# A list scheduler that plans VectorE's SBUF operations and GpSimd's operations in turns

## The chip, the cores and the metric

The kernel runs on one core of a Trainium2 chip. The core has a matrix engine (TensorE, PE in the profile), three engines for elementwise work (VectorE or DVE, ScalarE or ACT, GpSimd or POOL), an engine that issues most of the transfers (SyncE or SP), and 16 DMA engines. Each engine takes its own instructions strictly in the order in which the program lists them, and waits where one needs a result that is not there yet. The metric is the device time of one execution in microseconds, as the median of the runs. VectorE, ScalarE and TensorE reach the accumulators (PSUM, eight banks); GpSimd works in this kernel only between tiles of the on-chip memory (SBUF).

## What is computed

The reference is a windowed attention followed by a two-layer feed-forward block:

```python
scores = (1 / sqrt(64)) * q @ k.T            # 4 batches, 8 heads, 768 positions, 64 wide
keep = is_sink | ((rel >= 0) & (rel < 128))  # the first 4 positions, or the last 128
a = softmax(where(keep, scores, -1e9))
x = concat_heads(a @ v)                      # 3072 tokens x 512
h = x @ w_in                                 # 512 x 2048
g = h * sigmoid(1.702 * h)
out = g @ w_out                              # 2048 x 512, float32
```

All inputs are float32. The kernel casts them to float16 on the chip and accumulates in float32.

## The kernel before

The 3072 tokens are worked through in twelve blocks k = 0 to 11 of 256 tokens (three blocks make a batch). For each block and each of four pairs of heads p there is a *front*: q and k are cast to float16 (tiles qk), transposed on TensorE (L446), copied out of PSUM (qkT), multiplied to scores (L513), put through the exponential on ScalarE (L530, tiles at) and multiplied by a 0/1 mask on VectorE (L539, or L543 for the first block of a batch). Then there is a *back*: TensorE multiplies by v (L573), VectorE takes the reciprocal of the sums and scales (L587, L589, tiles xn), and TensorE transposes the result (L596) into xT. For the first block of a batch GpSimd also copies the keys and values of the sink positions (ks, L466, and vs, L422).

The first layer, `mm1`, multiplies xT by w_in in eight groups of eight matmuls per block (L630). Of each group ScalarE takes tanh (L642, tiles th), VectorE builds gT from th and the PSUM bank (L644), and the bank is free again. Three such banks rotate.

The second layer, `mm2`, multiplies gT by w_out. Blocks 0, 1 and 11 do so directly (L780). Blocks 2 to 10 use a scheme that replaces eight products of halves by seven (L705). It needs four tiles wt, which are sums and differences of quarters of w_out (`sums`, L650 to L660): 4 tiles x 4 pieces = 16 operations of 128 x 512 elements. A piece c needs the casts c and 4 + c of w_out, of eight. It also needs four sums of gT per block (sm, L675, on VectorE).

Weights come in as eight loads of 1 MB (w0 to w3 are w_in, w4 to w7 w_out, in the order w4, w6, w5, w7), each into one of four staging places that lie in the tiles gT and sm. Each load is followed by two casts of 128 x 1024 elements; all sixteen are on GpSimd (`CAST_W`). The casts of q, k and v are on GpSimd from k = 2 on; for k = 0 and 1 the planner may choose among engines (`CAST_QK`, `CAST_V`). All casts have one line in the profile, L263.

The order on every engine is found by a planner that runs before the kernel is built (`Plan.run`, L57). Each operation is given one or several engines with two planned times: how long it occupies the engine, and how long until its result is there. The planner keeps the time at which each engine is free, and takes operations one by one: for each engine it finds the earliest start, picks, among operations that could start within 20 ns of it, the one of the lowest priority number, and then takes the engine whose choice comes first. Where an operation may go to several engines, the later end counts against an engine (L120). Priorities are due times: `nominal(k, slot)` is 9000 + 16600 k + 16600 slot / 8 ns. The sums of w_out have the due time of k = 2; the casts of weights come before everything. The planned times in question are:

```python
"POOL": (n / 0.96 + 30, n / 0.96 + 130), "DVE": (n / 1.92 + 40, n / 1.92 + 155),   # casts of n
"ACT": (n / 1.2 + 60, n / 1.2 + 170)
SUM_W = {"POOL": (1000, 1100), "DVE": (340, 430)}                                  # a sum of w_out
```

so a cast of 1024 is planned with 1097 ns on GpSimd and 913 on ScalarE (results after 1197 and 1023), and a cast of 512 with 563 on GpSimd. In the plan every engine works on its own: an operation of VectorE takes the same planned time whether GpSimd is working or not. The planned times set only the order of the instructions; the waits on the chip follow from the data alone.

Of the kernel before, what the change touches and what calls it, by code (L numbers as in the profile page):

```python
# [35 lines left out]
LANES = 8  # L36

COLD = 4700.0
ENGINES = ("PE", "ACT", "DVE", "POOL", "SP")


class Plan:
# [14 lines left out]
    def run(self, warm=None, warm_until=0.0, late_bank=0.0):  # L57
        for o in self.ops:
            o.left = len(o.deps)
            for d in o.deps:  # L60
                d.users.append(o)
        free = {e: 0.0 for e in ENGINES}
        ready = {e: [o for o in self.ops if e in o.engs and not o.left] for e in ENGINES}

        bank_free = {b: 0.0 for b in range(self.n_banks)}
        if late_bank:
            bank_free[self.n_banks - 1] = late_bank

        count = {c: {i: 0.0 for i in range(n)} for c, n in self.limits.items()}
        dma_free = 0.0  # L70
        landed = []
        order = []
        todo = len(self.ops)

        def after(d, e):
            if d.eng != e or isinstance(d.engs[e][1], tuple):
                return d.end + HOP.get((d.eng, e), 50)
            return d.start + d.engs[e][0] + (0 if d.eng == "PE" else 60)

        def could(o, e):  # L80

            if o.behind and o.behind.start is None:
                return None, None
            s = max([free[e]] + [after(d, e) for d in o.deps])
            if isinstance(o.engs[e][1], tuple) and len(landed) >= LANES:
                s = max(s, landed[-LANES])
            if not o.acq:
                return s, s
            cls, n = o.acq
            times = sorted(bank_free.values())  # L90
            places = sorted(count[cls].values())
            if len(times) < n or len(places) < n:
                return s, None
            return s, max(s, times[n - 1], places[n - 1])

        while todo:
            best = None
            for e in ENGINES:
                found = sorted(
                    [(*could(o, e), o) for o in ready[e]], key=lambda x: (x[2].prio, x[2].seq)  # L100
                )
                keep, held_from = [], None
                for s0, s, o in found:
                    if s0 is None:
                        continue
                    if o.acq and o.acq[1] > 2 and (s is None or s > s0):

                        held_from = s0 if held_from is None else min(held_from, s0)
                        if s is not None:
                            keep.append((s, o))  # L110
                        continue
                    if s is None or (o.acq and held_from is not None and s >= held_from):
                        continue
                    keep.append((s, o))
                if not keep:
                    continue
                first = min(s for s, _ in keep)
                s, o = min(((s, o) for s, o in keep if s <= first + 20), key=lambda x: (x[1].prio, x[1].seq))
                lat = o.engs[e][1]
                key = s if len(o.engs) == 1 else s + lat - min(x[1] for x in o.engs.values())  # L120
                if best is None or key < best[0]:
                    best = (key, s, o, e)
            if best is None:
                raise RuntimeError("no operation can be planned")
            _, s, o, e = best
            dur, lat = o.engs[e]
            if e == "PE" and warm and s < warm_until:
                t = max(free["PE"], 300.0)
                while t + 110 < s:
                    order.append((t, -1, warm, e))  # L130
                    t += 107 if t < COLD else 57
            for x in o.engs:
                ready[x].remove(o)
            o.eng, o.start = e, s
            if o.acq:
                cls, n = o.acq
                o.banks, o.places = [], []
                for _ in range(n):
                    b = min((b for b in bank_free if bank_free[b] <= s), key=lambda b: (bank_free[b], b))
                    del bank_free[b]  # L140
                    o.banks.append(b)
                    p = min((p for p in count[cls] if count[cls][p] <= s), key=lambda p: (count[cls][p], p))
                    del count[cls][p]
                    o.places.append(p)
            free[e] = s + dur
            if isinstance(lat, tuple):
                dma_free = max(s + 2000, dma_free) + lat[0]
                o.end = dma_free + (500 if lat[0] < 500 else 1100)
                landed.append(o.end)
            else:  # L150
                o.end = s + lat
            for owner, i in o.rel:
                t = o.end + 80
                bank_free[owner.banks[i]] = t
                count[owner.acq[0]][owner.places[i]] = t
            for u in o.users:
                u.left -= 1
                if not u.left:
                    for x in u.engs:
                        ready[x].append(u)  # L160
            order.append((s, o.seq, o.fn, e))
            todo -= 1
        order.sort(key=lambda x: (x[0], x[1]))
        return [(fn, e) for _, _, fn, e in order]
# [7 lines left out]
def kernel(  # L172
# [38 lines left out]
    mask = pool.tile([P, 4 * P], FP16, name="mask")  # L211
# [7 lines left out]
    wt = {n: pool.tile([P, NH, HM], FP16, name=f"wt{n}") for n in "1234"}  # L219
# [36 lines left out]
    def cast(n, engs):  # L256

        ns = {"POOL": (n / 0.96 + 30, n / 0.96 + 130), "DVE": (n / 1.92 + 40, n / 1.92 + 155),
              "ACT": (n / 1.2 + 60, n / 1.2 + 170)}
        return pick(ns, engs)  # L260

    def copy(e, out, in_):
        {"POOL": nc.gpsimd.tensor_copy, "DVE": nc.vector.tensor_copy, "ACT": nc.scalar.copy}[e](out=out, in_=in_)  # L263
# [3 lines left out]
    def uses(name, slot, o):  # L267
        users.setdefault((name, slot), []).append(o)
# [38 lines left out]
    o_table = op("ACT", 1300, 1400, lambda: nc.scalar.activation(out=dummy, in_=zero[:, 0:8], func=AF.Exp),  # L307
                 [o_zero], prio=NEVER + 8, kind="const")

    CAST_W = ["POOL"] * 8  # L310
    CAST_QK = ["DVE ACT POOL", "DVE POOL"] + ["POOL"] * (NK - 2)
    CAST_V = ["POOL ACT DVE", "POOL ACT"] + ["POOL"] * (NK - 2)
    COPY = ["DVE ACT"] * NK
# [4 lines left out]
    def weights(n_th, j, at):  # L318
# [8 lines left out]
        for n in range(2):  # L327
# [3 lines left out]
            else:  # L331
                to, fr = w_out16[:, 4 * (j - 4) + 2 * n : 4 * (j - 4) + 2 * n + 2], dst[:, 2 * n : 2 * n + 2]
            o = plan.any(cast(1024, CAST_W[j]), lambda e, to=to, fr=fr: copy(e, to, fr), [o_l], prio=at, kind="cw")
            uses(*stage[n_th % RW][:2], o)
# [11 lines left out]
    def nominal(k, slot):  # L346
        return 9000.0 + k * L + slot * L / 8
# [302 lines left out]
    def sums():  # L650

        for n, x, y, alu in (("3", wq["22"], wq["12"], ALU.subtract), ("1", wq["12"], wq["11"], ALU.subtract),
                             ("2", wt["3"], wq["11"], ALU.add), ("4", wq["21"], wt["2"], ALU.subtract)):
            for c in range(4):
# [4 lines left out]
                deps = [o_wout[c], o_wout[NS // 2 + c]] + [o_wt[d, c] for d in {"2": "3", "4": "2"}.get(n, "")]  # L659
                o_wt[n, c] = plan.any(SUM_W, f, deps, prio=nominal(SEVEN_FROM, 0), kind="wt")  # L660

    SUM_W = {"POOL": (1000, 1100), "DVE": (340, 430)}
    o_sm = {}

    def mm2_seven(k):
# [215 lines left out]
```

## Time and profile before

| what | value |
|---|---|
| median of 3 runs | 236.49 us (236.44 to 236.9) |
| the profiled execution | 236.4 us, of it 234.7 us from the first to the last instruction |
| granted TensorE clock, mean | 0.992 |
| TensorE busy | 222.2 us |
| VectorE busy | 190.3 us in 412 instructions |
| ScalarE busy | 140.9 us in 293 instructions |
| GpSimd busy | 98.6 us in 163 instructions |
| the 16 casts of weights, all on GpSimd | 5.2 + 4.5 us (w_in), 4.4 + 4.1 us (w_out) |
| sums of w_out on VectorE, GpSimd | 15 and 1 |

The profile is one execution. Its page gives the busy time of each engine, then the span in 40 equal slices with a digit for the busy tenths of each, the clock that TensorE was granted (9 is full), the chain of work that ended last, and groups of instructions by line. A group shows line, engine, operation, tiles written and read, shape and count, then busy time and mean duration of one, then the idle time of its engine in front of it and what ended that. Matmuls overlap each other, so their durations are longer than their spacing, and a TensorE that is shown as busy is not at its peak.

### The profile page before, as it was taken

What the parts mean: (1) busy time and instruction counts of PE and PEld (TensorE: products, weight loads), DVE (VectorE), ACT (ScalarE), POOL (GpSimd) and SP (SyncE); (2) the same over time, 40 slices, a digit from 0 to 9 for tenths busy, and PEclk for the clock granted to TensorE, in tenths of its full rate; (3) what the DMA queues carried; (4) which work ended last, traced back from release to release, by engine and by line L of the source; (5) the groups of instructions that cost most, each with busy time, mean ns of one, the idle gap of its engine ahead of it and who ended that gap; (6) DMA issues with size and microseconds to landing.
All of it is one profiled execution on the core that took longest, in us unless ns stands there. A gap on an engine that the chain in (4) does not pass through costs nothing.

```text
span 234.7 us, 6390 instructions
## 1 busy us (share of the span) xinstructions
PE 222.2 (95%) x2534; PEld 183.0 (78%) x2534; DVE 190.3 (81%) x412; ACT 140.9 (60%) x293; POOL 98.6 (42%) x163
## 2 busy tenths in 40 slices
PE   8876999959999999999999999999999999999994
PEld 7654886526788888888789889888888888888863
DVE  6788979976899988988979879889969869878520
ACT  3749562536688838838648838838567757635320
POOL 5658889971899960358521441243300000000000
PEclk9999999979999999999999999999999999999999
DMA  6999999999879994644284004004003003003042
GB/s 169 292 357 387 382 383 287 288 302 274 223 191 295 250 232 90 176 100 89 74 197 92 0 3 89 4 1 94 0 13 82 0 14 78 3 17 78 0 92 89
DMA packets 45743, 33.98 MB, mean 145 GB/s; under 512 B 1552, under 2 KB 38672, under 8 KB 45712
## 3 DMA queue, kind: packets, MB, share of 16 engines
q1 hardware_dynamic: 44480, 32.90, 52.0%
q10 hardware_dynamic: 1232, 0.66, 1.0%
q8 instruction: 20, 0.33, 0.6%
q14 instruction: 11, 0.09, 0.1%
HBM read 27.26 MB, written 6.29 MB: 143 GB/s over the span
## 4 chain that ended last, share of the span: by engine, by line
PE 75%; DVE 17%; ACT 3%; DMA 2%; issue 1%; ACTq 0%
PE bank L630 29%; PE bank L705 22%; PE bank L780 6%; PE bank L573 5%; DVE wt L658 5%; PE bank L513 4%; PE bank L446 4%; DVE gT L644 3%; DVE sm L675 2%; PE bank L596 2%; DMA qk<-in_k_dram 2%; DVE at L539 2%; ACT at L530 2%; DVE at L543 1%; PE bank L474 1%
## 5 line engine op out<-in xcount | busy, mean ns | idle before, releaser
L630 PE MATMUL bank<-xT,w_in 128*128 128x256 f16 x768 | 101.7, 273 | 0.0
L642 ACT ACTIVATE th<-bank 128x512 f16<-128x512 f32 x96 | 57.6, 601 | 49.6 <-PE bank L630 46.0
L630 PEld LDWEIGHTS <-w_in 128*128 128x128 f16 x768 | 72.1, 98 | 10.3 <-issue 1.3
L644 DVE SCALAR_TENSOR_TENSOR gT<-th,bank 128x512 f16<-128x512 f16 x96 | 64.9, 679 | 9.0 <-ACT th L642 8.7
L530 ACT ACTIVATE at<-bank 128x512 f16<-128x512 f32 (+1 forms) x96 | 49.1, 569 | 11.8 <-PE bank L513 11.2
L263 POOL CAST qk<-qk 128x512 f16<-128x512 f32 (+1 forms) x42 | 28.9, 722 | 27.9 <-PE bank L446 25.7
L263 POOL CAST v<-v 64x512 f16<-64x512 f32 x43 | 30.3, 705 | 8.8 <-PE bank L573 6.4
L705 PE MATMUL bank<-wt,sm 128*128 128x256 f16 x216 | 30.6, 273 | 0.4 <-DVE sm L675 0.3
L705 PEld LDWEIGHTS <-sm 128*128 128x128 f16 x288 | 26.5, 98 | 4.8 <-DVE sm L675 0.9
L539 DVE TENSOR_TENSOR at<-at,mask 128x1024 f16<-128x1024 f16 x32 | 23.5, 753 | 6.6 <-ACT at L530 6.6
L780 PE MATMUL bank<-w_out,gT 128*128 128x512 f16 (+1 forms) x112 | 24.5, 358 | 0.0
L573 PE MATMUL bank<-v,at 128*128 128x65 f16 x352 | 21.5, 193 | 2.0 <-DVE at L539 1.8
L705 PEld LDWEIGHTS <-gT 128*128 128x128 f16 x216 | 20.1, 98 | 2.3 <-issue 0.3
L573 PEld LDWEIGHTS <-at 128*128 128x128 f16 x352 | 17.3, 97 | 4.0 <-DVE at L539 2.2
L589 DVE TENSOR_TENSOR xn<-bank,rcp 128x256 f16<-128x256 f32 x48 | 19.8, 417 | 0.4
L466 POOL COPY ks<-qkT 64x4 f16<-64x4 f16 x32 | 9.5, 297 | 24.8 <-ACT qkT L263 19.7
L705 PE MATMUL bank<-w_out,gT 128*128 128x256 f16 x144 | 19.7, 273 | 0.0
L446 PE MATMUL bank<-ident,qk 128*128 128x128 f16 x192 | 18.9, 225 | 0.5 <-DVE qk L263 0.4
L730 DVE SCALAR_TENSOR_TENSOR osb<-bank,osb 128x256 f32<-128x256 f32 x45 | 18.4, 409 | 0.6 <-PE bank L705 0.6
L482 ACT ACTIVATE ats<-bank 128x256 f16<-128x256 f32 x32 | 12.4, 388 | 9.2 <-PE bank L474 7.8
L446 PEld LDWEIGHTS <-qk 128*128 128x128 f16 x192 | 14.0, 100 | 3.1 <-DVE qk L263 1.1
L780 PEld LDWEIGHTS <-gT 128*128 128x128 f16 x112 | 10.9, 101 | 6.9 <-issue 1.3
(53 smaller groups left out, 274.4 us busy)
## 6 DMA issues: line engine op xcount, KB each, us to landing
v<-in_v_dram SPq DMA_DIRECT2D x12, 512.0 KB, 7.2
out_dram<-osb SPq DMA_DIRECT2D x45, 128.0 KB, 2.4
qk<-in_q_dram SPq DMA_DIRECT2D x11, 512.0 KB, 5.2
qk<-in_k_dram SPq DMA_DIRECT2D x11, 512.0 KB, 6.7
gT<-in_moe_w_in_dram SPq DMA_DIRECT2D x2, 1024.0 KB, 10.1
sm<-in_moe_w_in_dram SPq DMA_DIRECT2D x2, 1024.0 KB, 13.0
gT<-in_moe_w_out_dram SPq DMA_DIRECT2D x2, 1024.0 KB, 8.0
sm<-in_moe_w_out_dram SPq DMA_DIRECT2D x2, 1024.0 KB, 8.5
```

The costliest lines, as they stand in the source:

```text
L263: {"POOL": nc.gpsimd.tensor_copy, "DVE": nc.vector.tensor_copy, "ACT": nc.scalar.copy}[e](out=out, in_=in_)
L446: nc.tensor.transpose(ps[:, e, :, i, :], c16[:, i, e, 2 * p : 2 * p + 2].rearrange("s h d -> s (h d)"), ident)
L530: nc.scalar.activation(out=A[:, i, 0:W], in_=f32(o_s, 2 * n + i)[:, 0:W], func=AF.Exp, scale=scale)
L539: nc.vector.tensor_tensor(out=a_, in0=a_, in1=m_[:, 2 * P :].unsqueeze(1).to_broadcast((P, 4, 2 * P)), op=ALU.mult,)
L573: nc.tensor.matmul(avp()[:, j, i], a_, v_, start=(n == 0), stop=(n == len(mms) - 1))
L589: o_n = op("DVE", 333, 425, lambda: nc.vector.tensor_tensor(out=X[:, p].rearrange("s j (h d) -> s j h d", h=2), in0=avp()[:, :, :, 0:D], i ...
L630: nc.tensor.matmul(f32(holder[0])[:, bass.ts(e, TB)], w_in16[:, c, bass.ts(Fi, P)], X[:, c], start=(c == 0), stop=(c == NP - 1),)
L642: o_t = op("ACT", 477, 600, lambda first=first: nc.scalar.activation(out=th[first.places[0]], in_=f32(first), func=AF.Tanh, scale=0.851), ...
L644: o_g[k, s] = op("DVE", 595, 690, lambda first=first, s=s: nc.vector.scalar_tensor_tensor(out=g[:, 2 * s : 2 * s + 2].rearrange("p a t -> ...
L705: nc.tensor.matmul(f32(holder[bank_of])[:, 0:HM], x[:, Fi], w[:, Fi], start=first and Fi == 0, stop=Fi == NH - 1, skip_group_check=True)
L730: f, ns = (lambda: nc.vector.scalar_tensor_tensor(out=out, in0=src(), scalar=0.5, in1=add, op0=ALU.mult, op1=ALU.add)), (333, 425)
L780: nc.tensor.matmul(f32(holder[0])[:, 0:w], g[:, Fi, bass.ts(j, P)], w_out16[:, Fi, c], start=(n + h == 0), stop=(n + h == NS),)
```

## The change

Three things are changed.

1. The planner knows of a time up to which VectorE or GpSimd holds what both are thought to share (`held`). Every GpSimd operation holds it, and every VectorE operation whose kind is in `SHARED`: the masks, the sums of gT, the sums of w_out, and the casts of q, k and v. Such an operation can't be planned to start before the other engine's holding ends: for VectorE's at its start plus duration, for GpSimd's 130 ns before that. An operation that issues several instructions (the ks and vs copies, the mask's construction) holds for its whole planned time.
2. The sums of w_out may go only to VectorE.
3. The eight casts of w_out may go to GpSimd or ScalarE, by the plan's choice.

```diff
+SHARED = ("mask", "sum", "wt", "cqk", "cv")
...
+        held = {"DVE": 0.0, "POOL": 0.0}
...
+        def locks(o, e):
+            return e == "POOL" or e == "DVE" and o.kind in SHARED
 
         def could(o, e):
...
             s = max([free[e]] + [after(d, e) for d in o.deps])
             if isinstance(o.engs[e][1], tuple) and len(landed) >= LANES:
                 s = max(s, landed[-LANES])
+            if locks(o, e):
+                s = max(s, held["DVE" if e == "POOL" else "POOL"])
...
             dur, lat = o.engs[e]
+            if locks(o, e):
+                held[e] = s + dur - (130 if e == "POOL" else 0)
...
-    CAST_W = ["POOL"] * 8
+    CAST_W = ["POOL"] * 4 + ["POOL ACT"] * 4
...
-    SUM_W = {"POOL": (1000, 1100), "DVE": (340, 430)}
+    SUM_W = {"DVE": (340, 430)}
```

## The prediction

> **What bounds the kernel now.** I read the page's first two parts, then the windows around the weak slices, then the chain and the waits there. Shares and slices first:
>
> ```profile
> span 234.7 us, 6390 instructions
> PE 222.2 (95%) x2534; PEld 183.0 (78%) x2534; DVE 190.3 (81%) x412; ACT 140.9 (60%) x293; POOL 98.6 (42%) x163
> PE   8876999959999999999999999999999999999994
> POOL 5658889971899960358521441243300000000000
> PEclk9999999979999999999999999999999999999999
> ```
>
> TensorE is the bound nearly everywhere, so what counts is where it is not. Each slice is 5.87 us. After the start, one slice is weak: the 5 in PE's row, at 47 to 53 us, with the 7 of the clock beside it. GpSimd is full just before it. The windows around it:
>
> ```profile
> 36.00:50.00 14.00, 10.71 (x76) 6.32 (x76) 13.63 (x20) 5.24 (x10) 13.51 (x18) 1.00 1.15 285
> 60.00:80.00 20.00, 19.78 (x236) 15.81 (x234) 18.83 (x43) 16.27 (x35) 18.96 (x30) 1.00 1.00 253
> 50.00:51.00 1.00, 1.00 (x11) 0.66 (x9) 0.00 (x0) 0.00 (x0) 0.94 (x2) 0.50 1.21 301
> 51.00:52.00 1.00, 1.00 (x8) 0.70 (x6) 0.66 (x2) 0.73 (x2) 0.29 (x1) 0.50 1.18 317
> 52.00:53.00 1.00, 1.00 (x4) 0.34 (x3) 1.00 (x3) 0.63 (x2) 0.00 (x0) 0.50 1.03 348
> 53.00:54.00 1.00, 1.00 (x6) 0.45 (x5) 0.39 (x1) 0.03 (x1) 0.00 (x0) 0.85 0.64 169
> ```
>
> The columns are busy time of PE, weight loads, VectorE, ScalarE and GpSimd (instructions in brackets), then the granted clock. From 36 to 50 us VectorE is busy for 13.63 of 14 us, GpSimd for 13.51, TensorE for 10.71. From 50 to 53 us TensorE's clock is granted at 0.50, at 53 to 54 at 0.85: 3 x 0.50 + 0.15 = 1.65 us of work lost. The chain through this stretch names the work:
>
> ```profile
> 37.09 5.08 DVE wt L658 x6
> ...
> 42.76 0.73 DVE wt L658
> ...
> 44.09 3.33 DVE wt L658 x5
> ...
> 48.02 1.46 DVE wt L658 x2
> 49.48 0.35 DVE qkT L263
> 49.87 0.61 PE bank L513 x6
> ```
>
> The sums of w_out (L658, tiles wt) stand in VectorE's queue in runs of six, one, five and two, between gT operations. Behind the last stands the copy of qkT, and behind that copy TensorE's scores (L513). That wait among PE's waits in 33 to 54 us, then an earlier one in PE's timeline, then line L705's matmuls that read wt (the two last numbers before the form are the first and last start):
>
> ```profile
> PE bank L513 <- DVE qkT L263: 3.3, 1, 3.3
> ```
> ```profile
> 20.20 0.24 PE L573 MATMUL bank<-v,at 128*128 128x65 f16 x2 [1.80 <-DVE at L539]
> ```
> ```profile
> L705 PE MATMUL bank<-wt,sm x216: 269/273/283, 78.8 to 219.8; 128*128 128x256 f16 x108
> ```
>
> So the sums cost TensorE one stall of 3.3 us, and the half clock follows it. The stall of 1.8 us before 20.2 us was followed by none: the clock row of the page has 9 there. And nothing needs the sums at 49 us: their first reader starts at 78.8.
>
> **The price of one sum.** Two of line L658's three forms on VectorE (count, then minimum, median and maximum in ns), and the first sum in VectorE's timeline:
>
> ```profile
> L658 DVE TENSOR_TENSOR wt<-w_out x7: 411/811/1281, 34.8 to 45.1; 128x512 f16<-128x512 f16 x7
> L658 DVE TENSOR_TENSOR wt<-wt,w_out x4: 823/826/1253, 38.7 to 46.6; 128x512 f16<-128x512 f16 x4
> ```
> ```profile
> 34.83 0.55 DVE L658 TENSOR_TENSOR wt<-w_out 128x512 f16<-128x512 f16 x1
> ```
>
> The same shape takes 0.41 or 0.81 us. The plan puts it at 0.34. GpSimd meanwhile ran these:
>
> ```profile
> 29.25 2.03 POOL L263 CAST w_out<-gT 128x1024 f16<-128x1024 f32 x2 [0.65 <-DMA gT<-in_moe_w_out_dram]
> 31.95 2.03 POOL L263 CAST w_out<-gT 128x1024 f16<-128x1024 f32 x2 [0.67 <-DMA gT<-in_moe_w_out_dram]
> 33.95 1.15 POOL L658 TENSOR_TENSOR wt<-w_out 128x512 f16<-128x512 f16 x1
> 35.05 2.22 POOL L263 CAST w_out<-sm 128x1024 f16<-128x1024 f32 x2
> 37.43 2.22 POOL L263 CAST w_out<-sm 128x1024 f16<-128x1024 f32 x2 [0.16 <-DMA sm<-in_moe_w_out_dram]
> ...
> 45.72 2.74 POOL L263 CAST qk<-qk 128x512 f16<-128x512 f32 x4
> ...
> 57.49 1.45 POOL L466 COPY ks<-qkT 64x4 f16<-64x4 f16 x4 [6.19 <-ACT qkT L263]
> ```
>
> I read the 0.4 us between the two prices as VectorE waiting in front of a sum until GpSimd's instruction is done. The old plan counted none of it: 15 sums at 0.34 are 5.1 us in the plan; at 0.81 they are 12.2. VectorE's queue fell some 7 us behind, and what stood behind the sums came late.
>
> **The change part by part.**
>
> *Sums in turns with GpSimd.* The plan now starts such a VectorE operation only when no planned GpSimd operation runs, and the reverse. On the chip only the order within each queue changes, no wait is added. Of the 16 sums, eight need only the first two w_out loads. Seven of these ran on VectorE, one of them alone at 34.83 us and six in the chain's first run of 5.08 us: 0.55 + 5.08 = 5.6 us. With GpSimd's casts halved there (next part), I take eight at 0.41: 3.3 us, a gain of 2.3 us; at worst eight at 0.81 are 6.5, a loss of 0.9. The second eight took 0.73 + 3.33 + 1.46 = 5.5 us of the chain, beside qk and v casts that stay. They are bounded by eight at 0.41 (gain 2.2) and eight at 1.28 (loss 4.7); I take 0.73, the chain's price of the single one: 5.8 us, a loss of 0.3. Together VectorE gets 2.0 us back in a stretch where it has no idle time, so the stall of 3.3 us falls to 1.3. The sum that leaves GpSimd is in these eight and eight; GpSimd gets its 1.15 us.
>
> *The clock.* With 1.3 us of stall, less than the 1.8 that was followed by a full clock, the half clock goes: 1.65 us. It is kept if the stall stays near 3.3: bounds 0 and 1.65.
>
> *Half of the w_out casts on ScalarE.* The plan takes the engine that ends first. Two casts become ready with each landing; GpSimd's 1.20 us latency twice in a row loses to ScalarE's 1.02, so I expect one of each pair, four in all, on ScalarE. It has no such shape in the trace; from two of its casts and its spare time in 28 to 33 us:
>
> ```profile
> L263 ACT CAST v<-v 64x512 f16<-64x512 f32 x3 | 1.9, 621 | 0.1
> L263 ACT CAST qk<-qk 128x256 f16<-128x256 f32 x2 | 0.8, 404 | 0.1
> L642 ACT ACTIVATE th<-bank 128x512 f16<-128x512 f32 x6 | 3.5, 596 | 1.7 <-PE bank L630 1.0 <-DVE gT L644 0.7
> ```
>
> The slope is (621 - 404) / 256 = 0.85 ns an element, so 1024 take an estimated 621 + 512 x 0.85 = 1.06 us. Behind such a cast stand the tanh operations, and behind them VectorE's gT and the bank that the next L630 group needs. Two casts fall into 28 to 33 us: 2.1 us into 1.7 us of idle time, so 0.4 us of delay. Bounds: 0, and 2.1 plus 1.3 us of waiting for the landings that GpSimd now waits out (0.65 + 0.67). The other two fall at 35 and 37 us, where ScalarE was busy for 5.24 of 14 us: nothing. If its spare time were gone, they too would cost 2.1. They issue no DMA. GpSimd gets 4 x 1.02 us (2.03 / 2 each), which frees the staging tiles sooner; the DMA engines stayed busy there (share 1.15 in 36 to 50 us, the last column but one), so nothing lands sooner.
>
> *Start.* In the plan VectorE and GpSimd may no longer cast or mask together at k=0 and k=1 either. What it can win is bounded by two masks:
>
> ```profile
> 18.68 2.91 DVE L539 TENSOR_TENSOR at<-at,mask 128x1024 f16<-128x1024 f16 x2 [0.65 <-ACT at L530]
> ```
> ```profile
> L539 DVE TENSOR_TENSOR at<-at,mask 128x1024 f16<-128x1024 f16 x8 | 5.3, 683 | 2.1 <-ACT at L530 2.1
> ```
>
> These two took 2.91 us; the eight after 170 us, where GpSimd rests, take 0.68 each: 1.5 us at most. The masks have no other work to change places with, so I take 0; a loss up to the same 1.5 us, if one more mask meets a cast as those did.
>
> *The rest.* From 60 to 80 us VectorE and GpSimd are nearly full again, but TensorE is busy for 19.78 of 20: I take 0. [...]
>
> *Sum.* -2.0 - 1.65 + 0.4 = -3.25 us against the profiled execution's 236.4 us (span 234.7 and 1.7 around it): 233.15. The median of the three runs, 236.49, lies 0.09 above: 233.2 us. The stall that is left would be late for the same copy of qkT; next would be GpSimd's casts for k=3, which started at 45.7 us.
>
> **The rivals.** *The turns do not hold.* The change then does not do what it says. Nothing on the chip enforces the order that the plan assumes: if landings and durations drift by half a cast, each sum still meets one. Then 16 sums cost 0.81 in place of 15, +0.8 us on a VectorE without idle time, the stall and the half clock stay: 237.3 us. For it: the old plan missed VectorE by some 7 us in 15 us. Against it: half of the w_out casts leave GpSimd whatever the turns do. [...]
>
> *The sums go too late (slower).* In the plan a sum may start only in GpSimd's gaps, and masks or copies may take those. Place: 60 to 80 us, where VectorE has 20 - 18.83 = 1.17 us to spare. Price: N sums there at 0.81 us cost 0.81 N - 1.17, against a stall and clock gain of 3.3 + 1.65 - 0.4 = 4.55. It decides from N = 7 on; with N = 10 it is +2.4 us, 238.9. For it: GpSimd is busy for 18.96 us there. Against it: GpSimd rests for 6.19 us before 57.5 us, and a sum outranks whatever belongs to a later k.
>
> *More than forecast.* The stall goes wholly, ScalarE's casts are free and the start wins its 1.5 us: -3.3 - 1.65 - 1.5 = -6.45, 230.0 us.
>
> **How the numbers follow.** A change of 0.2% is 0.47 us, about the distance between the runs shown (236.44 to 236.9). Forecast, anything from 232 to 236: 0.50. More than that: 0.12. Gain and costs cancel, as with the second eight sums at 1.28 us: 0.07. Turns that do not hold: 0.14. Sums too late: 0.17. So faster 0.62, same 0.07, slower 0.31. The range 230.5 to 237.6 leaves out most of the late sums (0.13) and the end of the largest gain (0.05); the forecast's own range is 232 to 236.
>
> **What would show it.** Right: sums (L658) all on VectorE, singly between gT operations, the first eight near 0.41 us; four casts of w_out on ScalarE near 1.06 us; PE's wait for qkT in 33 to 60 us below 1.8 us; no window at clock 0.50 after 25 us. Wrong: sums at 0.81 in long runs again, tanh waiting behind ScalarE's casts in 28 to 33 us while PE waits for banks, sums behind 60 us, or a chain that is already late at 25 us.

## The result and the profile after

The changed kernel takes 234.59 us in the median of 7 runs (233.76 to 235.64), the kernel before 236.35 beside it (235.89 to 236.9). The ratio is 0.9927 with a 95% interval of [0.9904, 0.995]: faster by 0.7%, about 1.8 us. The forecast was 233.2. The profiled executions, from which the views below are read, took 236.4 us before and 235.64 us after, the longest of the seven, so that the traces show about half of the gain.

The page of the changed kernel, its span, busy times and three rows of slices. Lines after the edited places have moved: L640 is the old L630, L654 the old L644, L668 the old L658.

```profile
span 233.8 us, 6387 instructions
PE 221.6 (95%) x2536; PEld 184.0 (79%) x2536; DVE 189.7 (81%) x417; ACT 143.7 (61%) x294; POOL 91.3 (39%) x157
PE   7887599999999999999999999999999999999994
POOL 6658844882999960168521341142400000000000
PEclk9999979999999999999999999999999999999999
```

The weak slice has not gone, it has moved. PE's 5 at 47 to 53 us is a 9 now, and a new 5 stands at 23 to 29 us, with the 7 of the clock behind it. The windows of the two places, first before, then after (columns as in the prediction: PE, weight loads, VectorE, ScalarE, GpSimd, clock):

```profile
25.00:30.00 5.00, 5.00 (x51) 4.52 (x48) 3.94 (x11) 2.83 (x6) 4.14 (x5) 1.00 1.05 382
45.00:55.00 10.00, 6.71 (x62) 3.86 (x61) 7.06 (x14) 3.77 (x9) 6.07 (x9) 0.83 1.10 284
```
```profile
25.00:30.00 5.00, 3.07 (x29) 2.20 (x26) 3.87 (x10) 0.87 (x2) 4.34 (x5) 0.82 1.05 376
45.00:55.00 10.00, 9.75 (x92) 5.76 (x90) 8.40 (x17) 6.41 (x13) 6.57 (x9) 1.00 1.10 280
60.00:80.00 20.00, 19.79 (x241) 16.40 (x239) 18.67 (x42) 16.01 (x34) 19.09 (x30) 1.00 0.87 220
```

From 45 to 55 us TensorE does 92 matmuls in place of 62, from 25 to 30 us 29 in place of 51. To add this up, I count the matmuls that have started by a time, by shape, each once, and weigh each with its spacing where TensorE runs without gaps: 0.109 us for 256 columns (52 take 5.68 us in the chain of before), others in proportion to their columns, those of 65 columns 0.031 (their spacing in TensorE's timeline), and the scores, which are on 64 rows each, at half of their columns' share: they start in pairs 3 to 4 ns apart, and eight of them, 1536 columns together, from 63.65 to 63.94 us in the kernel before. Counted so, every trace ends with the same 203.2 us. This estimate of work done up to a time, in us (differences in the text are taken before rounding):

| up to | before | changed | turns from 26 us on | turns alone | price, no turns | price alone | turns and price |
|---|---|---|---|---|---|---|---|
| 25 us | 8.6 | 8.3 | 8.0 | 8.4 | 8.2 | 8.7 | 8.7 |
| 30 us | 13.5 | 10.1 | 12.9 | 11.6 | 13.2 | 13.7 | 10.8 |
| 45 us | 28.5 | 24.5 | 28.0 | 26.6 | 28.3 | 28.8 | 25.3 |
| 55 us | 33.2 | 33.7 | 36.8 | 36.4 | 36.5 | 36.7 | 35.2 |
| 80 us | 56.7 | 57.4 | 59.3 | 57.6 | 60.7 | 61.0 | 55.7 |

The first two columns are the result: 4.0 us lost up to 45 us, 4.5 won from 45 to 55. What is left, 0.5 us at 55 and 0.7 at 80, is carried to the end; the two profiled spans differ by 234.7 - 233.8 = 0.9 us. The other columns belong to the experiments.

Where it is won: the sums in the changed kernel (count, minimum, median, maximum in ns), and the chain around them.

```profile
L668 DVE TENSOR_TENSOR wt<-w_out x8: 410/504/831, 38.3 to 47.4; 128x512 f16<-128x512 f16 x8
L668 DVE TENSOR_TENSOR wt<-wt,w_out x4: 417/621/826, 42.0 to 48.9; 128x512 f16<-128x512 f16 x4
L668 DVE TENSOR_TENSOR wt<-w_out,wt x4: 412/680/828, 43.8 to 50.6; 128x512 f16<-128x512 f16 x4
```
```profile
43.84 1.95 DVE wt L668 x3
...
46.44 3.33 DVE wt L668 x5
...
50.36 1.09 DVE wt L668 x2
51.45 0.35 DVE qkT L273
51.83 0.40 PE bank L523 x6
```

The medians fell from between 0.81 and 0.83 us to between 0.50 and 0.68, though the sums still stand in rows of three, five and two, and TensorE's scores follow the copy of qkT without the 3.3 us of waiting. But they come at 51.83 us, where before they came at 49.87. Where it is lost: VectorE's timeline, then TensorE's.

```profile
18.57 0.69 DVE L549 TENSOR_TENSOR at<-at,mask 128x1024 f16<-128x1024 f16 x1 [0.61 <-ACT at L540]
19.86 0.18 DVE L597 RECIPROCAL rcp<-bank 128x4 f32<-128x4 f32 x1 [0.60 <-PE bank L583]
20.08 0.42 DVE L599 TENSOR_TENSOR xn<-bank,rcp 128x256 f16<-128x256 f32 x1
21.05 0.29 DVE L273 COPY xT<-bank 128x256 f16<-128x256 f16 x1 [0.55 <-ACT at L540]
21.25 4.43 DVE L549 TENSOR_TENSOR at<-at,mask 128x1024 f16<-128x1024 f16 x3
```
```profile
27.34 0.28 PE L606 MATMUL bank<-ident,xn 128*128 128x128 f16 x2 [1.66 <-DVE xn L599]
```

Before, the second of the four masks of k = 1 came right behind the first at 18.68 us. Now three of them stand behind the reciprocal, xn and xT of the first pair, for which VectorE waits 0.60 and 0.55 us, and then run in a row for 4.43 us: 1.5 us each, where a mask alone takes 0.68. The plan, printed with its planned starts in us, shows why:

```
before   masks 16.32 17.54 18.75 20.32    w_in casts on GpSimd 16.95 18.05 | 19.95 21.05
changed  masks 16.42 19.29 19.89 20.49    w_in casts on GpSimd 17.02 18.11 | 21.09 22.18
```

In the new plan the second mask gives way to the first two casts, then three masks use the pause, and the next two casts give way to them. On the chip nothing in the program holds the casts back but their data: GpSimd ran these four from 18.58 us in one row of 5.12 us, and the three masks met the last two and the next ones. In the three other traces with this order of the start (turns alone, turns up to 26 us, turns and price) the three masks took 3.08 to 3.56 us. The loss does not hang on one execution: in the four traces with this order TensorE has done 10.1 to 11.6 us of work at 30 us, in the ten whose start has the order of before 12.9 to 14.4.

### The profile page after: what moved, and what is told of

It is laid out like the page before. It is cut to its first block, busy times and chain, and to the rows that moved or that the text cites. A ratio compares the mean times of both kernels' runs of the same rounds, so it can differ in the third digit from the quotient of the medians.

```text
span 233.8 us, 6387 instructions
## 1 busy us (share of the span) xinstructions
PE 221.6 (95%) x2536; PEld 184.0 (79%) x2536; DVE 189.7 (81%) x417; ACT 143.7 (61%) x294; POOL 91.3 (39%) x157
## 4 chain that ended last, share of the span: by engine, by line
PE 67%; DVE 20%; DMA 4%; ACT 4%; POOL 2%; issue 1%; ACTq 0%; POOLq 0%
PE bank L640 28%; PE bank L715 20%; PE bank L790 5%; DVE gT L654 4%; PE bank L583 4%; DVE at L549 4%; PE bank L456 3%; PE bank L523 3%; DVE wt L668 3%; DVE sm L685 2%; ACT at L540 2%; DVE xn L599 2%; DMA qk<-in_k_dram 2%; DMA qk<-in_q_dram 2%; PE bank L606 2%
## 5 line engine op out<-in xcount | busy, mean ns | idle before, releaser
L640 PE MATMUL bank<-xT,w_in 128*128 128x256 f16 x768 | 103.7, 275 | 0.0
L652 ACT ACTIVATE th<-bank 128x512 f16<-128x512 f32 x96 | 57.4, 600 | 47.7 <-PE bank L640 43.4
L640 PEld LDWEIGHTS <-w_in 128*128 128x128 f16 x768 | 72.2, 99 | 10.5 <-issue 1.4
L654 DVE SCALAR_TENSOR_TENSOR gT<-th,bank 128x512 f16<-128x512 f16 x96 | 64.9, 680 | 10.9 <-ACT th L652 10.2
L540 ACT ACTIVATE at<-bank 128x512 f16<-128x512 f32 (+1 forms) x96 | 49.3, 570 | 11.1 <-PE bank L523 10.8
L273 POOL CAST qk<-qk 128x512 f16<-128x512 f32 (+1 forms) x42 | 28.0, 695 | 29.1 <-PE bank L456 25.3
L273 POOL CAST v<-v 64x512 f16<-64x512 f32 x42 | 29.1, 693 | 10.4 <-PE bank L583 7.4
L715 PEld LDWEIGHTS <-sm 128*128 128x128 f16 x288 | 27.1, 98 | 4.6 <-DVE sm L685 0.7
L715 PE MATMUL bank<-wt,sm 128*128 128x256 f16 x216 | 29.7, 273 | 0.6 <-DVE xT L273 0.6
L549 DVE TENSOR_TENSOR at<-at,mask 128x1024 f16<-128x1024 f16 x32 | 24.8, 785 | 6.7 <-ACT at L540 6.7
L790 PE MATMUL bank<-w_out,gT 128*128 128x512 f16 (+1 forms) x112 | 23.2, 349 | 0.0
L476 POOL COPY ks<-qkT 64x4 f16<-64x4 f16 x32 | 9.5, 298 | 24.5 <-DVE qkT L273 18.0
L715 PE MATMUL bank<-w_out,gT 128*128 128x256 f16 x144 | 18.8, 273 | 0.0
L456 PEld LDWEIGHTS <-qk 128*128 128x128 f16 x192 | 13.4, 98 | 3.4 <-DVE qk L273 1.7
L606 PE MATMUL bank<-ident,xn 128*128 128x128 f16 x96 | 13.3, 220 | 2.7 <-DVE xn L599 2.6
## 6 DMA issues: line engine op xcount, KB each, us to landing
gT<-in_moe_w_in_dram SPq DMA_DIRECT2D x2, 1024.0 KB, 10.1
```

Of the source, the lines that this page charges most:

```text
L456: nc.tensor.transpose(ps[:, e, :, i, :], c16[:, i, e, 2 * p : 2 * p + 2].rearrange("s h d -> s (h d)"), ident)
L540: nc.scalar.activation(out=A[:, i, 0:W], in_=f32(o_s, 2 * n + i)[:, 0:W], func=AF.Exp, scale=scale)
L549: nc.vector.tensor_tensor(out=a_, in0=a_, in1=m_[:, 2 * P :].unsqueeze(1).to_broadcast((P, 4, 2 * P)), op=ALU.mult,)
L640: nc.tensor.matmul(f32(holder[0])[:, bass.ts(e, TB)], w_in16[:, c, bass.ts(Fi, P)], X[:, c], start=(c == 0), stop=(c == NP - 1),)
L652: o_t = op("ACT", 477, 600, lambda first=first: nc.scalar.activation(out=th[first.places[0]], in_=f32(first), func=AF.Tanh, scale=0.851), ...
L654: o_g[k, s] = op("DVE", 595, 690, lambda first=first, s=s: nc.vector.scalar_tensor_tensor(out=g[:, 2 * s : 2 * s + 2].rearrange("p a t -> ...
```

## The experiments

All ratios are against the kernel before on the same chip, with 95% intervals. In a diff, "-" is the kernel named in the text, and constants are written out.

**Turns from 26 us on.** Against the changed kernel:

```diff
+TURNS_FROM = 26000.0
-            if locks(o, e):
+            if locks(o, e) and s > TURNS_FROM:
                 s = max(s, held["DVE" if e == "POOL" else "POOL"])
```

> The changed kernel, but the planner counts the turns only for operations that could start after 26 us of planned time, so the order of the first 25 us is again that of before. Theory A (the change won about 4.8 us of TensorE work between 45 and 55 us by shorter sums and lost about 4 us at 21 to 30 us, where three masks were planned behind one another): the loss goes, the gain stays, 230.5 us (229.5 to 232). Rival B (the stall at 46 us was not removed, it was only hidden because TensorE arrived there late): the stall of 3 us and the half clock come back with the early start, 234.5 to 236 us.

Measured: 233.34 us, 0.9876 [0.9817, 0.9934]. PE's only wait from 33 to 60 us that the view lists, and a later window:

```profile
PE bank L485 <- DVE qkT L274: 0.7, 1, 0.7
```
```profile
70.00:80.00 10.00, 9.40 (x123) 7.86 (x121) 10.00 (x21) 6.91 (x16) 9.59 (x14) 1.00 1.04 264
```

The order of the start is that of before and the stall does not return: rival B falls. But theory A's 230.5 was not reached either. At 55 us this run is 3.1 us of work ahead of the changed kernel, at 80 us 1.9: from 70 to 80 us VectorE is never idle and TensorE is, for 0.6 us. More than a third of the lead is gone by then; at the end of the two profiles it is 233.8 - 231.4 = 2.4 us. This run differs in one more thing: its plan gave five casts of w_out to ScalarE, the changed kernel's four.

**The other half: turns only up to 26 us.** The changed kernel with

```diff
-            if locks(o, e):
+            if locks(o, e) and s < 26000.0:
                 s = max(s, held["DVE" if e == "POOL" else "POOL"])
```

> The changed kernel with the turns counted only for operations that could start before 26 us of planned time: the other half of the run with turns from 26 us on. If the start's loss is the turns' work alone: TensorE is 3 to 4 us behind at 30 us as in the changed kernel. Theory A (late turns shorten the sums): they go back to about 0.8 us each and the time is 235.5 to 237. Theory C (the casts on ScalarE do it, the late turns add nothing): the same as the changed kernel, 234.5 us.

Measured: 236.13 us, 0.998 [0.9947, 1.0014]: no faster than before. The two longest of PE's waits from 25 to 85 us, and the first form of the sums:

```profile
PE bank L607 <- DVE xn L600: 2.1, 3, 1.7
PE bank L485 <- DVE qkT L274: 1.7, 1, 1.7
```
```profile
L669 DVE TENSOR_TENSOR wt<-w_out x8: 411/654/1257, 37.7 to 46.6; 128x512 f16<-128x512 f16 x8
```

The start's loss is there with these turns alone. Without the late turns the changed kernel's gain (0.9927) is gone, though the intervals touch; theory C is not borne out. The sums did not go back to 0.8 us, as A had it, but stayed between.

**The turns alone.** The changed kernel with the other two edits undone:

```diff
-    CAST_W = ["POOL"] * 4 + ["POOL ACT"] * 4
+    CAST_W = ["POOL"] * 8
-    SUM_W = {"DVE": (340, 430)}
+    SUM_W = {"POOL": (1000, 1100), "DVE": (340, 430)}
```

> The turns in the plan alone; the sums and the casts of w_out may go where they could before. Theory A: the loss at the start comes whole (4 us); of the gain only what the turns bring, since GpSimd has all eight casts of w_out and each sum meets one: 236 to 238 us, sums near 0.7 us each. Rival B: the late start hides the stall here too, 234.5 us as in the changed kernel.

Measured: 236.11 us, 1.0014 [0.9977, 1.005]: the same as before. It loses less at the start than expected (1.9 us of work at 30 us), and its half clock comes earlier than the changed kernel's, as the window shows (clock 0.57 in the mean):

```profile
20.00:24.00 4.00, 4.00 (x33) 2.93 (x28) 2.83 (x6) 2.54 (x7) 3.15 (x4) 0.57 1.05 386
```

It has no stall at 46 us and is 3.3 us of work ahead of before at 55. It has only 0.9 left at 80. Its plan put all sums on VectorE although it could have done otherwise, so this run is the change without the casts on ScalarE.

**The casts alone.** The kernel before with one line:

```diff
-    CAST_W = ["POOL"] * 8
+    CAST_W = ["POOL"] * 4 + ["POOL ACT"] * 4
```

> The casts of w_out on GpSimd or ScalarE alone, no turns in the plan. Theory A: the start is that of before; the sums of the first half meet fewer casts, so half of the gain of 4.8 us: 234 us (233 to 235), stall at 46 us about half. If the turns carry the whole gain: 236 to 236.5 us, the same as before.

Measured: 234.79 us, 0.9926 [0.989, 0.9961]: as fast as the whole change. PE's longest wait from 20 to 65 us:

```profile
PE bank L474 <- DVE qkT L263: 2.4, 1, 2.4
```

The stall is shorter and still there. With the casts moved, the plan put three sums on GpSimd in place of one, so that VectorE had 13 to do; the run does not tell the two effects apart.

**All sums on VectorE alone.** The kernel before with one line:

```diff
-    SUM_W = {"POOL": (1000, 1100), "DVE": (340, 430)}
+    SUM_W = {"DVE": (340, 430)}
```

> All sums on VectorE alone. One sum more of 0.4 to 0.8 us on a VectorE without idle time: 236.5 to 237.3 us by theory A, the stall at 46 us longer by as much. If GpSimd's sum of 1.15 us was what held up the casts behind it, 235.5 us.

Measured: 237.1 us, 1.0033 [0.9996, 1.0069]. The wait at 46 us among PE's:

```profile
PE bank L513 <- DVE qkT L263: 3.5, 1, 3.5
```

The stall of before, 0.2 us longer. Alone this part wins nothing.

**A price in place of turns.** The kernel before, with the casts of the change and the sums planned at about what they took:

```diff
-    CAST_W = ["POOL"] * 8
+    CAST_W = ["POOL"] * 4 + ["POOL ACT"] * 4
-    SUM_W = {"POOL": (1000, 1100), "DVE": (340, 430)}
+    SUM_W = {"DVE": (800, 890)}
```

> No turns at all; casts of w_out as in the change, all sums on VectorE, but planned with 800 ns in place of 340, near what they took before. Theory D (what matters is that the planner knows how long a sum takes, so that it does not put a row of them in front of more urgent work): no stall of TensorE at 46 us and the start of before, 233.3 us like the run with turns from 26 us on. If the turns are needed, sums stay at 0.8 us: 234.8 us like the casts alone, or worse, 236, since four of the sums now come after 50 us.

Measured: 231.03 us, 0.977 [0.9726, 0.9814]: the fastest of all, ahead of the changed kernel by more than both intervals. The sums and two windows:

```profile
L658 DVE TENSOR_TENSOR wt<-w_out x8: 416/419/828, 35.5 to 45.1; 128x512 f16<-128x512 f16 x8
L658 DVE TENSOR_TENSOR wt<-wt,w_out x4: 415/658/830, 40.2 to 48.2; 128x512 f16<-128x512 f16 x4
L658 DVE TENSOR_TENSOR wt<-w_out,wt x4: 387/405/829, 49.5 to 56.9; 128x512 f16<-128x512 f16 x4
```
```profile
36.00:50.00 14.00, 14.00 (x105) 8.31 (x104) 11.17 (x20) 9.62 (x18) 11.43 (x16) 1.00 1.14 282
60.00:80.00 20.00, 20.00 (x244) 17.11 (x242) 18.89 (x40) 15.86 (x34) 18.65 (x28) 1.00 1.14 284
```

With 800 ns a sum no longer fits every gap in the plan. The last four run behind 49 us, masks and copies of the next block go first, and two of the three forms run at 0.41 to 0.42 us in the median, though nothing in this plan knows of turns. VectorE has 2.8 us of idle time from 36 to 50 us in place of 0.4. What theory D named came, no stall and the start of before, at a time below its 233.3. Whether a later due time for the sums, at their old price, would do the same was not tried.

**The price alone.** The kernel before with one line, the casts of w_out on GpSimd as they were:

```diff
-    SUM_W = {"POOL": (1000, 1100), "DVE": (340, 430)}
+    SUM_W = {"DVE": (800, 890)}
```

> The kernel before with one edit: all sums on VectorE, planned with 800 ns in place of 340. Casts of w_out stay on GpSimd. If the price alone does it, no stall of TensorE at 46 us: 232 to 233 us. If the casts on ScalarE are half of the gain of the run with both (231.0 us): 233.5 us. If sums at 0.8 us are too much for VectorE without the casts' relief: 235 to 236.

Measured: 232.7 us, 0.9843 [0.9797, 0.9889]. The price is the larger part of that gain. Whether the casts on ScalarE bring the rest, about 0.7%, is not shown: the two intervals overlap, the two traces have nearly the same work done at 80 us (61.0 and 60.7 us), and five of the six runs here had a mean granted clock of 0.993 or less, against two of the six with the casts.

**A price of 560 ns.** The fastest kernel with

```diff
-    SUM_W = {"DVE": (800, 890)}
+    SUM_W = {"DVE": (560, 650)}
```

> The run with the price and without turns, with sums planned at 560 ns, half way between 340 and 800. In that run the three forms of the sums took 0.42, 0.66 and 0.41 us in the median, so 560 is near what they cost there. If a price near the true cost is enough: 231 us, no stall of TensorE at 46 us. If the price must be high so that sums give way to everything else: 233 us, between the casts alone (234.8) and the price of 800 (231.0).

Measured: 232.54 us, 0.9861 [0.9815, 0.9907].

```profile
L658 DVE TENSOR_TENSOR wt<-w_out x8: 411/804/1260, 34.8 to 43.8; 128x512 f16<-128x512 f16 x8
```

No stall at 46 us either, but the sums of this form (line L658's view) are back at 0.8 us in the median, and it is slower than with 800. What a sum costs depends on where the price puts it; the price of 800 put it where it cost less than that.

**Turns and price.** The changed kernel with

```diff
-    SUM_W = {"DVE": (340, 430)}
+    SUM_W = {"DVE": (800, 890)}
```

> The changed kernel with the sums planned at 800 ns. If the turns' start costs 3 to 4 us whatever comes behind it, TensorE is that much behind at 30 us and the time is 234 to 235, 3 to 4 us more than the same edit without turns (231.0). If the price repairs the changed kernel too: 231 to 232.

Measured: 237.17 us, 1.0041 [1.001, 1.0073]: 6 us slower than the same edit without turns. PE's waits from 20 to 65 us and the last four sums:

```profile
PE bank L606 <- DVE xn L599: 2.5, 3, 1.7
PE bank L583 <- DVE at L549: 2.0, 2, 1.2
```
```profile
L668 DVE TENSOR_TENSOR wt<-w_out,wt x4: 417/418/418, 54.2 to 55.2; 128x512 f16<-128x512 f16 x4
```
```profile
POOL ks L476 <- DVE qkT L273: 7.4, 1, 7.4
```

The start loses 2.6 us of work by 30 us. The sums run late, the last four at their lowest price, and still 3.0 us of work are lost from 55 to 80 us against the kernel before. The front of k = 3 comes late there: GpSimd waits 7.4 us for its first qkT (the third fence, from the waits in 50 to 80 us) and copies it at 58.54 us. But before it waited 6.19 us and copied at 57.49, so this is 1 us of the three; where the rest is lost is open. The turns do not only fail to add to the price, they undo it.

**The loss at 70 to 80 us.** Three runs looked for it. One takes the first, turns from 26 us on, and ends them at 50 us:

```diff
-            if locks(o, e) and s > TURNS_FROM:
+            if locks(o, e) and 26000.0 < s < 50000.0:
```

> Turns counted only for operations that could start between 26 and 50 us of planned time. If the turns after 50 us cost something by their order, the loss at 70 to 80 us shrinks: 232.5 us. If they do nothing there: 233.3 us. If they help: 234 us or more.

Measured: 232.12 us, 0.9795 [0.9745, 0.9845]. The other leaves the turns from 26 us on and lets the casts of k = 4 to 6 go to ScalarE:

```diff
-    CAST_QK = ["DVE ACT POOL", "DVE POOL"] + ["POOL"] * (NK - 2)
+    CAST_QK = ["DVE ACT POOL", "DVE POOL"] + ["POOL"] * 2 + ["POOL ACT"] * 3 + ["POOL"] * (NK - 7)
-    CAST_V = ["POOL ACT DVE", "POOL ACT"] + ["POOL"] * (NK - 2)
+    CAST_V = ["POOL ACT DVE", "POOL ACT"] + ["POOL"] * 2 + ["POOL ACT"] * 3 + ["POOL"] * (NK - 7)
```

> Turns from 26 us on as before, and the casts of q, k and v for k = 4 to 6 may go to ScalarE too (nine of 24 do). Theory E (the gain is given back at 70 to 80 us, where VectorE is never idle and its masks and gT sums meet GpSimd's casts): those operations fall towards 0.68 us, TensorE gets 0.5 to 1 us more done there, 232.5 us. If GpSimd is not the cause, or ScalarE's tanh waits behind the casts: 233.3 us or worse, 234.

Measured: 233.88 us, 0.9855 [0.9801, 0.9908], no better than without. Its profiled execution took 231.32 us, the fastest of its runs (up to 235.56), so its trace does not speak for it. The same edit on the fastest kernel:

> The run with the price and without turns, and casts of q, k and v for k = 4 to 6 that may go to ScalarE. If VectorE still loses to GpSimd's casts at 60 to 80 us: 230.3 us. As TensorE is already never idle there: 231.0, no change, or worse where tanh waits behind a cast.

Measured: 232.54 us, 0.9853 [0.9805, 0.9901]: slower than without it (0.977), though the intervals just overlap. So the turns after 50 us are more likely a cost than a help (0.9795 against 0.9876, intervals that overlap), and fewer casts on GpSimd do not bring it back. What takes 1 us of the lead between 55 and 80 us is not settled.

## Why the prediction was right

The sign and the range were right, the size was half: 1.8 us in place of 3.3. That the time fell into the range is in part luck. From 45 to 55 us 4.5 us of work were won, where the sums and the clock were to give 3.65; at the start 4.0 were lost, where nothing was forecast; and the casts alone, meant as a help, gave as much as the whole. By its steps:

*The sums.* Right, nearly to the number, in VectorE's timeline of the changed kernel: the first eight took 0.92 + 0.74 + 0.75 + 1.28 = 3.7 us of VectorE (forecast 3.3), the second eight 0.82 + 1.91 + 1.57 + 1.16 = 5.5 (forecast 5.8). The gain is 11.1 - 9.2 = 1.9 us; forecast 2.0.

*The stall.* Gone in the changed kernel, by more than forecast. But there TensorE came 2 us late, so that this alone is no proof. The run with turns from 26 us on is: there it comes early and waits 0.7 us in place of 3.3 (forecast 1.3).

*The clock.* At 50 to 53 us the half clock went, as forecast. In the profiled execution it came back at another place:

```profile
28.00:29.00 1.00, 1.00 (x8) 0.79 (x7) 0.82 (x3) 0.00 (x0) 0.61 (x1) 0.61 1.06 395
29.00:30.00 1.00, 1.00 (x14) 0.82 (x11) 0.09 (x1) 0.27 (x1) 0.73 (x1) 0.50 1.05 369
30.00:31.00 1.00, 1.00 (x11) 0.76 (x9) 0.57 (x3) 0.33 (x1) 0.31 (x1) 0.50 1.05 393
31.00:32.00 1.00, 1.00 (x9) 0.79 (x8) 0.62 (x2) 0.04 (x1) 0.04 (x1) 0.68 1.07 385
```

That costs 0.39 + 0.50 + 0.50 + 0.32 = 1.7 us, as much as was saved, and 0.7% of the span. So a mean granted clock of 0.993 or less goes with one such stretch or more: the twelve profiled executions with such a mean, of fourteen, each show one, the other two, at 0.999 and 1.00, show none. It does not come every time. Of the seven executions of the changed kernel two had a mean of 1.00 (233.76 and 234.59 us) and five 0.991 to 0.993; of the 74 executions of the kernel before that were timed beside the experiments none had more than 0.993. So the step held in two executions of seven. The reason given, that a stall below 1.8 us leaves the clock whole, was wrong: here the longest wait was 1.66.

*The casts on ScalarE.* Four, at the estimated size (1.06):

```profile
L273 ACT CAST w_out<-gT 128x1024 f16<-128x1024 f32 x2 | 2.1, 1046 | 0.0
L273 ACT CAST w_out<-sm 128x1024 f16<-128x1024 f32 x2 | 2.1, 1038 | 0.0
```

Their cost of 0.4 us cannot be seen in a run: with the casts alone nothing is lost up to 45 us (28.8 us of work, before 28.5). That they would be worth as much as the whole change was not foreseen; the forecast had them only as a help for the sums.

*The start.* This is the term that failed: it was taken as 0, with bounds of 1.5 us, and measured 3.3 us of work at 30 us and 4.0 at 45, of which the half clock is 1.7. The sentence that failed is "the masks have no other work to change places with". They did change places, with the reciprocal, xn and xT behind them. The bound was read from two masks that met a cast; it did not ask what the plan does with a cast that it believes it can hold back.

*The rivals.* That the turns do not hold is half true. At the start they do not hold, and the order that was built on them is what costs; with the turns up to 26 us alone the time is that of before. Beside the sums they are not needed: a higher price does the same and more. In the changed kernel the last two of the four casts from 18.58 us on, planned behind the three masks, ran among them, and each of these masks took 1.5 us. The sums did not go too late in the changed kernel; they came later when turns and price came together, the last at 55.2 us, still before the 60 us at which that rival put its harm; the fastest kernel's last sum came at 56.9, so lateness alone does no harm there.

*The signs.* Of those named for right, the four casts near 1.06 us and the wait for qkT below 1.8 us came. The sums did not come singly, and a window at clock 0.50 stands after 25 us. Of those named for wrong, the late chain came, five us later than named: TensorE is 0.3 us of work behind at 25 us and 3.3 at 30.

## What to carry to other kernels

A planner that orders queues should use only delays that the chip will really impose. One that lets engine A wait for engine B, where no semaphore makes it wait, puts A's queue into an order for a machine that is not there; at this kernel's start that cost two to three us of work. The cheaper repair here was to plan the operation at the time that it was seen to take, above what it then took, so that it gave way to more urgent work. And a change of planning rules is felt everywhere that the rule applies, so look at the first stage of the kernel as closely as at the one that it was made for.

## What the runs showed of the hardware

Operations on the same data type and shape took 0.41 or 0.81 us on VectorE: the sums in the kernel before, and again in the fastest kernel, where the first form took 0.42 in the median and 0.83 at most. A mask of 0.68 us took 1.5 beside casts of 1024 elements (the three from 21.25 us on in the changed kernel). In the traces of the kernel before and the changed one every sum of 0.7 us or more overlaps GpSimd's work for nine tenths of its time or more, in the fastest one's for more than six tenths; but the kernel before's sum of 0.41 us at 44.02 us does so too, for 0.96 of its time, and six of the fastest kernel's ten sums below 0.5 us do for more than six tenths (counted in the traces). So in these three traces no sum is that long without the overlap, and the overlap does not decide it alone. That VectorE waits for GpSimd there, as the prediction read it and the planner's `held` takes it, is not shown: no run took GpSimd's work away altogether.

TensorE's clock fell to 0.50 after a longest wait of 1.66 us in the changed kernel, and did not fall after one of 1.80 in the kernel before. The busy time around these differs: in 4 us of the changed kernel up to the fall (at 28.2 us), and then in 4 us of the kernel before around the wait of 1.80,

```profile
24.00:28.00 4.00, 1.78 (x23) 1.26 (x24) 3.97 (x9) 0.60 (x1) 4.00 (x4) 1.00 1.04 374
```
```profile
17.00:21.00 4.00, 2.20 (x37) 1.25 (x32) 3.05 (x4) 4.00 (x10) 2.43 (x2) 1.00 1.05 387
```

TensorE was busy for 1.78 and for 2.20 of 4 us. The busy time parts these two places in the order of their clocks, which the waits do not, but it does not part all traces. Ten of the kernels have the same planned order on every engine up to 24 us. Five of them show a half clock between 14.8 and 24.4 us, the other five, the kernel before among them, none; the price without turns and the kernel before from 14 to 19 us, with clocks of 0.66 and 1.00:

```profile
14.00:19.00 5.00, 4.39 (x41) 2.75 (x42) 2.87 (x7) 3.36 (x8) 2.46 (x4) 0.66 1.05 385
14.00:19.00 5.00, 3.51 (x42) 2.00 (x42) 3.24 (x11) 3.58 (x9) 1.94 (x3) 1.00 1.04 383
```

In the run with turns from 26 us on, the clock fell at 21.0 us though TensorE had been busy for more than 2.4 of any 4 us from 8 us on, more than the 2.2 after which it stayed full in the kernel before; from 20 to 25 us its matmuls of L641 took 382 ns in the mean, against 273 from 200 to 220 us. Whether a given pause brings the half clock thus differs from execution to execution here, and no rule for it is shown. Its length was 3.4 to 3.5 us in eleven of the twelve traces that have one (read in steps of 0.1 us), and 6.9 in the twelfth, turns from 26 to 50 us.
